# Batch 0's P turned and scaled by one matrix product with a diagonal, and the first layers ranked 16 units later

## The chip, the cores and the metric

One core of one Trainium2 chip runs the whole kernel. The metric is the device time of one execution in microseconds; of three runs of the kernel before, the median was 913.38 us (910.81 to 913.5). TensorE (PE) multiplies matrices, VectorE (DVE) and ScalarE (ACT) work on tiles in SBUF and PSUM, GpSimd (POOL) on tiles in SBUF, SyncE (SP) issues DMAs. PEld is TensorE's loading of the operand that stays in the array while the other one streams through it.

## The reference, cut to what matters

```python
B, H, S, D = 8, 8, 576, 64                    # float32 throughout
scores = q @ k.transpose(0, 1, 3, 2) / sqrt(D)
mask   = (arange(S)//64)[:, None] >= (arange(S)//64)[None, :]
scores = where(mask, scores, -1e9); scores -= scores.max(-1, keepdims=True)
P      = exp(scores); P = P / (P.sum(-1, keepdims=True) + 1e-9)
x      = (P @ v).transpose(0, 2, 1, 3).reshape(4608, 512)
h      = maximum(maximum(x @ w1, x @ w2), x @ w3)      # 512 -> 768
out    = h @ w_out                                     # 768 -> 512
```

## The kernel before

**Attention.** It runs by pairs of heads: 8 batches of 4 pairs, 32 pairs. Of the 576 query rows of a head, tiles t = 0 to 3 hold 128 rows each and see 128(t+1) keys; the last 64 rows of both heads share one tile, p4 (576 keys). A pair takes: first scores of tiles 3, 2 and 0 on TensorE (`qk`, L900, 12 records; a float32 matmul leaves two records), then p4 (`qk4`, L907) and tile 1 (L900 again); the row maximum on VectorE (`top`, L443); exp with row sums on ScalarE (`exp`, L606, and L926 for p4); 1/sum on VectorE (L735, L739; L937, L943 for p4); scaling of P by 1/sum on ScalarE or GpSimd (`normalise`, L459, L461); a turn of P, since the product with v needs keys in the partitions; and P times v (`pv`, L966).

**Batch 0.** The turn has two forms. Batches 1 to 7 transpose 32 x 32 blocks on VectorE (L626) and move them by DMA. Batch 0 (its Part is `PLAIN`) turns q, k (L812) and P (`raise_p` L560, `raise4` L952) on TensorE, in PE's transpose mode, 128 x 128 at a time: 25 such blocks in a pair, 100 in the batch. The result stands in PSUM (tiles named sb, five banks for all of attention) and is copied to the tile pz or pt by ScalarE or VectorE (`copy`, L251 and L253). Scores of one pair want four free banks.

**MoE.** Float32 values are split in a high and a low fp32r part, and each product is three matmuls. x of a batch is split into xh (ScalarE) and xl (GpSimd or VectorE, L256); a chunk is 512 rows, nine of them: one of each batch, and one for the last 64 rows of all. A chunk has 216 matmuls of the first layer (L1089, the maximum at L1102) and 72 of the second (L1123), whose operands are split into tiles hh and hl (slot "hi", three buffers). Weights come as 18 units for the first layer and 6 for the second, and are split on chip: a unit is five VectorE steps (L331, L338, L344, L355, L365), a few ScalarE copies and, in the first 18, four TensorE records (L371, L371, L372, L373).

**Order.** Every step is a `job` with a planner's cost for each engine, a rank and what it waits for. `in_order` plays the jobs through in advance: on every engine the job of the lowest rank that is ready comes first, and that gives each engine's order; the chip then runs it in that order, with waits. A pair of batch 0 is 14 ranks behind the last (`FIRST_PAIR`), later ones 24 (`PAIR`). The first layer of a batch's chunk starts at the rank where the batch's pairs end plus `END`; weight unit u has rank 28 + 3.5 u. Which of two engines takes a copy or a scaling also comes out of this play.

Of the kernel before, what the change touches and what calls it, by code (L numbers as in the profile page):

```python
# [9 lines left out]
F32 = mybir.dt.float32  # L10
# [145 lines left out]
def kernel(  # L156
# [29 lines left out]

    SECOND = 9
    NEAR = 4
    END = 24
    N = 512  # L190

    slots = dict(
# [270 lines left out]
    class Head:  # L463
# [5 lines left out]
        def plan(self, t0):  # L469

            pair, part, self.exps, self.inv = self.pair, self.pair.part, {}, {}
            for n, ts in enumerate(part.groups):
                apart, r = None, t0 + (SECOND if part.beside and ts == part.later else n)
                for t in ts:
                    m = P * (t + 1)
                    d = job(
                        {"DVE": dve(m) + 35.0},
                        r + 1,
                        self.top,
                        t,  # L480
                        after=(pair.scored[ts], apart, pair.began),
                        take=("stat",) if pair.began is None else (),
                    )
                    pair.began = pair.began or d
                    if t != ts[-1]:
                        apart = job({}, 0, lambda eng: None, after=(d,), lasts=GAP)
                    self.exps[t] = job({"ACT": act(m) + 200.0}, r + 2, self.exp, t, after=(d,), take=(f"p{t}",))
                join([self.exps[t] for t in ts], BANK)

        def turns(self, t0, after):  # L490

            pair, part, self.scales = self.pair, self.pair.part, {}
            for t in part.tiles:
                r = t0 + 8 + t / 2 + (SECOND if part.beside and t in part.later else 0)
                self.scales[t] = job(norm_cost(P * (t + 1)), r, self.scale, t, after=(self.inv[t],))
# [13 lines left out]
            return first  # L509

        def plain_turns(self, t0):

            pair, part = self.pair, self.pair.part
            heads, gate = pair.heads, None
            self.placed = []
# [12 lines left out]
            for t in part.tiles:  # L528
                up = job(
                    {"PE": RAISE * (t + 1)},  # L530
                    t0 + 12,
                    self.raise_p,
                    t,
                    after=(self.scales[t], gate),
                    take=("sb",) if gate else ("sb", pair.tag),
                )
                gate = self.gate = gate or up
                join((up,), (f"p{t}",))
                join((place(self.place, t, n=P * (t + 1), after=up),), ("sb",))
            if True:  # L540
                if self.j == 0:
                    pair.raised = [
                        job({"PE": RAISE * n}, t0 + 12, pair.raise4, a, after=(pair.scaled, gate), take=("sb",))
                        for a, n in ((0, 4), (1, 1))
                    ]
                    join(pair.raised, ("p4",))
                for a, n in ((0, 256), (1, 64)):
                    place(self.place4, a, n=n, after=pair.raised[a])
                if self.j == 1:
                    for a in range(2):  # L550
                        join([h.placed[-2 + a] for h in heads], ("sb",))
            self.moved = join(self.placed, ())
# [87 lines left out]
    class Pair:  # L640
# [11 lines left out]
        def plan(self, first, before):  # L652
# [63 lines left out]
            for r, ts in ((first + 7, [t for g in part.first for t in g]), (first + SECOND + 5, part.later)):  # L716
# [10 lines left out]
            join([x for h in self.heads for x in h.scales.values()], ("stat",))  # L727
# [13 lines left out]
        def plan4(self, first, tq, last):  # L741
            asked = job({"ACT": 510.0}, first - TURN + 2, self.ask, after=(tq,), take=("q8",))
            tops = []
            for a in range(2):
                last = job({"PE": 4 * pe(64 if a else 512)}, first + 3 + a, self.qk4, a, after=(asked, last), take=BANK)
                tops.append(
                    job(
                        {"DVE": dve(64 if a else 512) + 65.0},
                        first + 4 + a,
                        self.top4,  # L750
                        a,
# [1 line left out]
                        take=() if a else ("stat4",),  # L753
                    )
                )
            e = job({"ACT": act(512) + act(64) + 350.0}, first + 5, self.exp4, after=tops, take=("p4",), give=2 * BANK)
            inv = job({"DVE": SMALL}, first + 6, self.sum4, after=(e,), lasts=SMALL + GAP)
            inv = job({"DVE": SMALL}, first + 6, self.inverse4, after=(inv,))
            self.scaled = job(norm_cost(S), first + 7, self.scale4, after=(inv,), give=("stat4",))
            join((last,), ("q8",))  # L760
            return last

# [182 lines left out]
        def raise4(self, eng, a):  # L945

            z = self.ps[a] = psa.tile([P, P if a else 512], F32, name="sb")
            for c in range(1 if a else 4):
                src = self.p4[:, c * P : c * P + P]
                if a:  # L950
                    src = self.p4[:, 512:640]
                nc.tensor.transpose(z[:, c * P : c * P + P], src, plus.bitcast(F32))  # L952

        def scale4(self, eng):
            rs = self.stat[2][:, 0:1]
            normalise(eng, self.p4[:, 0:S], rs)
            if self.part.plain:
                nc.gpsimd.tensor_copy(self.p4[:, S:640], self.p4[:, 512:S])

        def pv(self, eng, half):  # L960

# [239 lines left out]
```

## Time and profile before

| | us |
|---|---|
| median of 3 runs (lowest, highest) | 913.38 (910.81, 913.5) |
| profiled execution, its own time | 915.56 |
| its span, first to last instruction | 913.8 |
| TensorE busy in it | 877.1 |
| VectorE busy | 566.3 |
| ScalarE busy | 447.1 |
| GpSimd busy | 184.0 |

Of 36.7 us in which TensorE is not busy, 24.3 lie in the first 103.5 us, where batch 0 runs nearly alone and the weights are split. A busy stretch counts to the modelled end of its last record, so a short burst counts longer than its records hold the array; the distance from start to start is the better price of one record. Clock means the clock granted to TensorE, as a share of 2.4 GHz.

### The profile page before, as it was taken

How to read it: one execution, taken by the hardware profiler on the slowest of the kernel's cores; microseconds unless marked ns; L12 is line 12 of the kernel's file. 1: busy time of each engine (PE TensorE's matmuls, PEld its weight loads, DVE VectorE, ACT ScalarE, POOL GpSimd, SP SyncE). 2: the span in 40 equal slices, each digit the busy share in tenths (PEclk: the TensorE clock that was granted, in tenths of full speed). 3: DMA queues.
4: the chain of work that ended last, by engine and by line, in shares of the span. 5: the costliest groups of instructions: out<-in, count | busy, mean ns of one | idle time of the engine just before them, and what ended most of it. 6: DMA issues, size and time to landing. Idle time of an engine off the chain costs nothing.

```text
span 913.8 us, 13405 instructions
## 1 busy us (share of the span) xinstructions
PE 877.1 (96%) x4336; PEld 643.2 (70%) x4336; DVE 566.3 (62%) x1534; ACT 447.1 (49%) x1227; POOL 184.0 (20%) x232
## 2 busy tenths in 40 slices
PE   5887999998999999999999999999999999999997
PEld 4544566775677777777777777777776778788886
DVE  4988999867767476656675766566656762122121
ACT  5687667655455545545444554545545542113012
POOL 3544213321122112111212121212111210001000
PEclk9998999998999999999999999999999999999999
DMA  5486336655555565546653665266535543000002
GB/s 116 124 230 167 75 83 193 134 133 123 111 114 121 119 138 111 115 97 151 130 111 81 129 141 124 78 131 129 121 96 125 112 86 94 12 1 35 12 1 46
DMA packets 221638, 97.10 MB, mean 106 GB/s; under 512 B 185216, under 2 KB 213888, under 8 KB 221568
## 3 DMA queue, kind: packets, MB, share of 16 engines
q1 hardware_dynamic: 203840, 81.30, 40.2%
q0 software_dynamic: 3456, 12.58, 4.2%
q10 hardware_dynamic: 14272, 2.36, 1.4%
q8 instruction: 34, 0.56, 0.3%
q14 instruction: 36, 0.29, 0.1%
HBM read 40.89 MB, written 9.44 MB: 55 GB/s over the span
## 4 chain that ended last, share of the span: by engine, by line
PE 87%; DVE 8%; ACT 2%; issue 2%; DMA 1%; POOL 0%; ACTq 0%; SPq 0%; DVEq 0%
PE pm L1089 47%; PE pm L1123 16%; PE sb L966 9%; PE sb L900 8%; PE sb L907 3%; DVE sb L443 2%; PE pm L371 1%; PE sb L560 1%; DVE pz L626 1%; DVE wo L344 1%; DVE kq L884 1%; ACT p L606 1%; ACT p L926 1%; DVE wo L338 1%; DVE wo L355 1%
## 5 line engine op out<-in xcount | busy, mean ns | idle before, releaser
L1089 PE MATMUL pm<-xh,w 128*128 128x512 f32 x1296 | 435.8, 405 | 1.0 <-ACT xh L251 1.0
L1089 PEld LDWEIGHTS pm<-xh,w 128*128 128x128 f32 x1296 | 244.7, 189 | 67.2 <-issue 14.1
L1089 PE MATMUL pm<-xl,w 128*128 128x512 f32 x648 | 254.5, 393 | 1.7 <-POOL xl L256 1.7
L606 ACT ACTIVATE p<-sb,nm 128x512 f32<-128x512 f32 (+3 forms) x256 | 133.2, 526 | 100.2 <-DVE nm L443 96.9
L461 POOL TENSOR_TENSOR p<-p,rs 128x128 f32<-128x128 f32 (+3 forms) x138 | 96.7, 724 | 312.5 <-DVE rs L739 265.1
L443 DVE CUSTOM_DVE_ANT_0 sb<-sb,mask 128x512 f32<-128x512 f32 (+3 forms) x288 | 142.9, 528 | 26.5 <-PE sb L907 11.8
L1102 DVE TENSOR_TENSOR m<-pm,m 128x512 f32<-128x512 f32 x108 | 74.1, 686 | 136.8 <-PE pm L1089 136.5
L626 DVE STREAM_TRANSPOSE pz<-p 128x512 f32<-128x512 f32 x280 | 135.7, 523 | 25.6 <-ACT p L459 17.2
L1089 PEld LDWEIGHTS pm<-xl,w 128*128 128x128 f32 x648 | 122.6, 189 | 31.0 <-issue 5.7
L1123 PE MATMUL pm<-wo,hh 128*128 128x512 f32 x432 | 134.5, 393 | 0.4 <-ACT hh L251 0.4
L900 PE MATMUL sb<-kq 64*128 64x128 f32 (+3 forms) x512 | 92.5, 472 | 5.6 <-ACT kq L251 1.8
L966 PE MATMUL sb<-pt,vn 128*64 128x320 f32 (+2 forms) x840 | 92.5, 361 | 3.6 <-issue 2.0
L1123 PEld LDWEIGHTS pm<-wo,hh 128*128 128x128 f32 x432 | 80.1, 188 | 17.7 <-ACT hh L251 0.8
L966 PEld LDWEIGHTS sb<-pt,vn 128*64 128x64 f32 x840 | 56.2, 137 | 44.3 <-issue 11.8
L1123 PE MATMUL pm<-wo,hl 128*128 128x512 f32 x216 | 84.4, 391 | 0.7 <-DVE hl L256 0.7
L900 PEld LDWEIGHTS sb<-kq 64*128 64x128 f32 x512 | 49.2, 192 | 48.1 <-issue 25.0
L251 ACT COPY m<-pm 128x512 f32<-128x512 f32 x54 | 31.6, 586 | 84.5 <-PE pm L1089 84.2
L884 DVE STREAM_TRANSPOSE kq<-nat 128x1152 f32<-128x1152 f32 x28 | 38.5, 1376 | 54.4 <-PE sb L900 53.1
L251 ACT CAST hh<-m 128x384 fp32r<-128x384 f32 x72 | 35.1, 511 | 75.6 <-PE pm L1123 44.2
L459 ACT ACTIVATE p<-p,rs 128x512 f32<-128x512 f32 (+3 forms) x118 | 64.4, 576 | 10.8 <-DVE rs L739 9.7
L256 DVE TENSOR_TENSOR hl<-m,hh 128x384 fp32r<-128x384 f32 x51 | 34.6, 679 | 27.2 <-ACT hh L251 26.2
L606 ACT ACTIVATION_READ_ACCUMULATOR p<-sb,nm 128x1 f32 x256 | 50.7, 198 | 0.0
(86 smaller groups left out, 724.2 us busy)
## 6 DMA issues: line engine op xcount, KB each, us to landing
pt<-pz SPq DMA_DIRECT2D x224, 200.0 KB, 3.9
w<-in_moe_w_dram POOLq DMA_DIRECT2D x18, 512.0 KB, 5.9
vn<-in_v_dram SPq DMA_DIRECT2D x64, 128.0 KB, 2.4
out_dram<-osb SPq DMA_DIRECT2D x32, 256.0 KB, 2.0
nat<-in_k_dram SPq DMA_DIRECT2D x112, 72.0 KB, 2.4
nat<-in_q_dram SPq DMA_DIRECT2D x96, 72.0 KB, 2.4
wo<-in_moe_w_out_dram POOLq DMA_DIRECT2D x6, 512.0 KB, 4.5
nat<-in_q_dram ACTq DMA_DIRECT2D x16, 72.0 KB, 3.3
```

The lines of the kernel that those rows point to most:

```text
L251: nc.scalar.copy(dst, src)
L443: nc.vector.tensor_tensor_reduce(out=ps, in0=ps, in1=hidden, scale=-SCALE, scalar=first, op0=ALU.add, op1=ALU.min, accum_out=out_)
L459: nc.scalar.mul(p, p, r)
L461: nc.gpsimd.tensor_tensor(out=p, in0=p, in1=r.broadcast_to([P, p.shape[1]]), op=ALU.mult)
L606: nc.scalar.activation(dst, src, AF.Exp, bias=nm[:, c : c + 1], scale=-1.0, accum_out=sm[:, c : c + 1])
L626: nc.vector.transpose(dst, p[:, 0 : n * P])
L884: nc.vector.transpose(kq.rearrange("p a s -> p (a s)"), nat.rearrange("p a s -> p (a s)"))
L900: nc.tensor.matmul(ps, self.q[h.own, P * t : P * (t + 1)], self.k[h.own, 0:w], start=True, stop=True)
L966: nc.tensor.matmul(o[h.own].rearrange("p (i u) -> p i u", u=n)[:, :, c0 : c0 + z - a], self.vn[:, kt, h.j, :], h.pt[:, :, a:z], start=(m = ...
L1089: nc.tensor.matmul(self.ps, w[i, f][:, c, :], xx, start=(c == 0 and s == 0), stop=(c == NC - 1 and s == 2))
L1102: nc.vector.tensor_tensor(out=m, in0=ps, in1=m, op=ALU.max)
L1123: nc.tensor.matmul(self.po, h, w[f], start=(f == 0 and s == 0), stop=(f == NF - 1 and s == 2))
```

## The change

In batch 0 no P is scaled any more. Instead a diagonal matrix with 1/sum on its diagonal is made for every tile of rows (`scaling`: the identity `plus` times 1/sum, on VectorE or GpSimd), three tiles of a head or two of tile 1 at a time and one for p4, and P is turned by an ordinary float32 product with it, P being the operand that is loaded: P^T times the diagonal is the turned and scaled P. Four such diagonal jobs stand in a pair. Their tiles are the hh and hl of the MoE's second layer and share its three buffers; a hh goes to the first head and then to tile 1, the hl to the second head. `scale4` keeps only the copy of p4's last 64 columns. The planner's prices change with it: the turn on TensorE costs twice as much, and the maximum and exp, of all batches, cost more (by 121 and 91 ns in `top` and `exp`). `END` goes from 24 to 40. Batches 1 to 7 run the same instructions as before, in another order.

```diff
-    END = 24
+    END = 40
...
-                        {"DVE": dve(m) + 35.0},
+                        {"DVE": dve(m) + 156.0},
...
-                    self.exps[t] = job({"ACT": act(m) + 200.0}, r + 2, self.exp, t, after=(d,), take=(f"p{t}",))
+                    self.exps[t] = job({"ACT": act(m) + 291.0}, r + 2, self.exp, t, after=(d,), take=(f"p{t}",))
...
             pair, part, self.scales = self.pair, self.pair.part, {}
+            if part.plain:
+                return self.plain_turns(t0)
             for t in part.tiles:
...
-            if part.plain:
-                return self.plain_turns(t0)
...
-                    {"PE": RAISE * (t + 1)},
+                    {"PE": 2 * RAISE * (t + 1)},
...
-                    after=(self.scales[t], gate),
+                    after=(pair.diags[t, self.j], gate),
...
-                        job({"PE": RAISE * n}, t0 + 12, pair.raise4, a, after=(pair.scaled, gate), take=("sb",))
+                        job({"PE": 2 * RAISE * n}, t0 + 12, pair.raise4, a, after=(pair.scaled, pair.diags[4, 0], gate), take=("sb",))
...
-                nc.tensor.transpose(z[:, c * P : c * P + P], p[:, c * P : c * P + P], plus.bitcast(F32))
+                nc.tensor.matmul(z[:, c * P : c * P + P], p[:, c * P : c * P + P], self.pair.diag[t, self.j], start=True, stop=True)
...
+            if part.plain:
+                self.diags = {}
+                d = None
+                for n, own in enumerate(([(t, 0) for t in (3, 2, 0)], [(t, 1) for t in (3, 2, 0)], [(1, 0), (1, 1)], [(4, 0)])):
+                    m = P * len(own)
+                    inv = self.inv4 if n == 3 else self.heads[0].inv[own[0][0]]
+                    d = job({"DVE": dve(m), "POOL": pool(m)}, first + 8, self.scaling, n, after=(inv, d), take=("hi",) if n in (0, 2) else ())
+                    self.diags.update(dict.fromkeys(own, d))
...
-            normalise(eng, self.p4[:, 0:S], rs)
             if self.part.plain:
                 nc.gpsimd.tensor_copy(self.p4[:, S:640], self.p4[:, 512:S])
+            else:
+                normalise(eng, self.p4[:, 0:S], rs)
+
+        def scaling(self, eng, n):
...
+            r = r.rearrange("p (n o) -> p n o", o=1).broadcast_to([P, len(own), P])
+            {"DVE": nc.vector, "POOL": nc.gpsimd}[eng].tensor_tensor(out=dst, in0=one, in1=r, op=ALU.mult)
```

TensorE, from the turn of the second pair's q and k (L812, after it L831) to the scores of that pair; L560 and L952 are the turn of the first pair's P, and p_147, p_154, p_164 or p_162, p_202 or p_209 its first head. Before:

```order
L812 MATMUL sb<-plus,nat 128x128 x9
L560 MATMUL sb<-plus,p_147 128x128 x4
L560 MATMUL sb<-plus,p_154 128x128 x3
L560 MATMUL sb<-plus,p_164 128x128
L952 MATMUL sb<-plus,p_170 128x128 x4
L560 MATMUL sb<-plus,p_202 128x128 x2
L952 MATMUL sb<-plus,p_170 128x128
L560 MATMUL sb<-plus,p_157 128x128 x4
L560 MATMUL sb<-plus,p_166 128x128 x3
L560 MATMUL sb<-plus,p_177 128x128
L560 MATMUL sb<-plus,p_207 128x128 x2
L900 MATMUL sb<-kq 128x512 x2
```

The same place after (L564 and L971 are the products, hh and hl the diagonals):

```order
L831 MATMUL sb<-plus,nat 128x128 x9
L564 MATMUL sb<-hh,p_147 128x128 x4
L564 MATMUL sb<-hh,p_154 128x128 x3
L564 MATMUL sb<-hh,p_162 128x128
L564 MATMUL sb<-hl,p_157 128x128 x4
L564 MATMUL sb<-hl,p_166 128x128 x3
L564 MATMUL sb<-hh,p_209 128x128 x2
L971 MATMUL sb<-hh,p_170 128x128 x5
L564 MATMUL sb<-hl,p_177 128x128
L564 MATMUL sb<-hh,p_222 128x128 x2
L919 MATMUL sb<-kq 128x512 x2
```

The 25 blocks of a pair stand in the same gap between two pairs' scores, seven of the second head ahead of tile 1 and p4 now.

GpSimd, from the copy in p4 of the first pair (L958, after it L976) on; L461 scales P, L303 asks for a weight unit. Before:

```order
L958 COPY p_170<-p_170 128x64
L461 TENSOR_TENSOR p_164<-p_164,rs 128x128
L461 TENSOR_TENSOR p_147<-p_147,rs 128x512
L461 TENSOR_TENSOR p_177<-p_177,rs 128x128
L461 TENSOR_TENSOR p_166<-p_166,rs 128x384
L461 TENSOR_TENSOR p_157<-p_157,rs 128x512
L303 DMA w_266<-in_moe_w_dram 128x4x256
```

After (L990 makes a diagonal):

```order
L976 COPY p_170<-p_170 128x64
L990 TENSOR_TENSOR hh<-plus,rs 128x384
L990 TENSOR_TENSOR hl<-plus,rs 128x384
L303 DMA w_254<-in_moe_w_dram 128x4x256
```

Five scalings of P have gone and two diagonals stand in their place, ahead of the second weight unit's request.

TensorE, around the first scores of the fifth pair (the first of batch 1), in the stage of the fourth pair's turn. Before:

```order
L1089 MATMUL pm<-xh_818,w_351 128x512
L900 MATMUL sb<-kq 128x512 x2
L900 MATMUL sb<-kq 128x384 x2
L900 MATMUL sb<-kq 128x128 x2
L371 MATMUL pm<-wo_696,plus 128x512
L372 MATMUL pm<-w_865,osb 128x512
L373 MATMUL pm<-wo_836,plus 128x512
L371 MATMUL pm<-wo_718,plus 128x512
L372 MATMUL pm<-w_885,osb 128x512
L373 MATMUL pm<-wo_869,plus 128x512
L560 MATMUL sb<-plus,p_744 128x128 x4
L560 MATMUL sb<-plus,p_747 128x128 x3
```

After:

```order
L564 MATMUL sb<-hh,p_797 128x128 x2
L371 MATMUL pm<-wo_704,plus 128x512
L372 MATMUL pm<-w_859,osb 128x512
L373 MATMUL pm<-wo_836,plus 128x512
L971 MATMUL sb<-hh,p_848 128x128 x5
L564 MATMUL sb<-hl,p_764 128x128 x4
L564 MATMUL sb<-hl,p_776 128x128 x3
L371 MATMUL pm<-wo_711,plus 128x512
L372 MATMUL pm<-w_904,osb 128x512
L373 MATMUL pm<-wo_889,plus 128x512
L919 MATMUL sb<-kq 128x512 x2
L919 MATMUL sb<-kq 128x384 x2
```

Before, the fifth pair's scores stand ahead of the whole turn of the fourth; after, 22 of the 25 products stand ahead of them.

## Rows read from the trace of the kernel before

**Rows 1.** The page's head and two of its 40 slices' rows.

```profile
span 913.8 us, 13405 instructions
...
PE   5887999998999999999999999999999999999997
...
PEclk9998999998999999999999999999999999999999
```

**Rows 2.** By stage: us, busy time (and records) of each engine, TensorE's clock, DMA.

```profile
0.00:23.90 23.90, 14.02 (x63) 10.01 (x63) 10.24 (x35) 12.52 (x37) 7.42 (x20) 0.93 0.52 123
23.90:62.10 38.20, 30.48 (x184) 18.61 (x184) 34.83 (x102) 28.41 (x84) 18.48 (x23) 1.00 0.68 184
62.10:83.40 21.30, 18.04 (x87) 9.41 (x86) 19.87 (x54) 16.69 (x44) 12.62 (x14) 1.00 0.50 123
83.40:103.50 20.10, 16.64 (x81) 9.69 (x81) 17.26 (x47) 13.79 (x39) 5.44 (x7) 0.83 0.39 120
103.50:134.80 31.30, 30.82 (x139) 20.70 (x135) 30.07 (x74) 19.64 (x48) 4.16 (x5) 1.00 0.42 95
134.80:215.00 80.20, 75.41 (x371) 54.46 (x372) 65.74 (x171) 48.28 (x128) 26.01 (x28) 0.97 0.56 142
215.00:780.00 565.00, 562.82 (x2857) 414.46 (x2856) 360.63 (x1019) 286.13 (x811) 104.83 (x133) 1.00 0.53 116
```

**Rows 3.** TensorE in time, 45 to 62 us and 31 to 33 us.

```profile
53.21 1.82 PE L560 MATMUL sb<-plus,p 128*128 128x128 f32 x12
...
31.58 0.43 PE L907 MATMUL sb<-kq,q 128*128 128x64 f32 x2
31.85 1.08 PE L371 MATMUL pm<-wo,plus 128*128 128x512 f32 x2
```

**Rows 4.** TensorE in time, 4 to 104 us: start, us, what, [idle before].

```profile
19.04 1.97 PE L560 MATMUL sb<-plus,p 128*128 128x128 f32 x8 [2.01 <-POOL p L461]
...
36.01 2.00 PE L900 MATMUL sb<-kq 64*128 64x512 f32 x12 [1.38 <-ACT kq L251]
...
62.10 2.00 PE L900 MATMUL sb<-kq 64*128 64x512 f32 x12
...
74.98 3.02 PE L900 MATMUL sb<-kq 64*128 64x512 f32 x12
...
81.99 0.60 PE L560 MATMUL sb<-plus,p 128*128 128x128 f32 x4
84.25 0.90 PE L560 MATMUL sb<-plus,p 128*128 128x128 f32 x3 [1.66 <-DVE pt L253]
...
93.06 0.38 PE L560 MATMUL sb<-plus,p 128*128 128x128 f32 x2
```

**Rows 5.** Scalings and copies: groups of the first 95 us; GpSimd in time; the page.

```profile
L461 POOL TENSOR_TENSOR p<-p,rs 128x384 f32<-128x384 f32 x5 | 5.0, 1006 | 3.6 <-DVE rs L739 3.6
...
L459 ACT ACTIVATE p<-p,rs 128x512 f32<-128x512 f32 x3 | 2.1, 709 | 0.0
...
L253 DVE COPY pt<-sb 128x512 f32<-128x512 f32 x4 | 2.8, 688 | 0.2 <-PE sb L560 0.2
...
17.58 3.54 POOL L461 TENSOR_TENSOR p<-p,rs 128x128 f32<-128x128 f32 x5
...
L256 DVE TENSOR_TENSOR hl<-m,hh 128x384 fp32r<-128x384 f32 x51 | 34.6, 679 | 27.2 <-ACT hh L251 26.2
```

**Rows 6.** GpSimd in time, 92 to 106 us, and VectorE, 36 to 104 us.

```profile
101.61 1.27 POOL L256 TENSOR_TENSOR xl<-x,xh 128x512 fp32r<-128x512 f32 x1 [2.29 <-ACT xh L251]
...
97.19 0.42 DVE L355 TENSOR_SCALAR wo<-wo 128x512 int32<-128x512 int32 x1
...
101.66 1.50 DVE L355 TENSOR_SCALAR wo<-wo 128x512 int32<-128x512 int32 x1
```

**Rows 7.** As Rows 2, two short stretches of lowered clock.

```profile
84.00:88.00 4.00, 3.75 (x10) 2.36 (x10) 2.34 (x8) 2.68 (x8) 0.31 (x1) 0.50 0.96 325
...
216.00:220.00 4.00, 4.00 (x15) 2.78 (x12) 3.71 (x13) 2.56 (x8) 0.08 (x1) 0.52 0.84 130
```

More of the change, by code (lines that the diff above doesn't have):

```diff
@@ L514, in plain_turns @@
             heads, gate = pair.heads, None
-            self.placed = []
+            self.placed, ups = [], {}
             def place(call, *args, n, after):
@@ L533, in plain_turns @@
                     t,
-                    after=(self.scales[t], gate),
+                    after=(pair.diags[t, self.j], gate),
                     take=("sb",) if gate else ("sb", pair.tag),
                 )
-                gate = self.gate = gate or up
+                gate, ups[t] = gate or up, up
                 join((up,), (f"p{t}",))
@@ L551, in plain_turns @@
                         join([h.placed[-2 + a] for h in heads], ("sb",))
+            self.ups = ups
+            if self.j == 1:
+                join([x for h in heads for x in h.ups.values()] + pair.raised, ("hi",))
+                join([h.ups[t] for h in heads for t in (3, 2, 0)], ("hi",))
             self.moved = join(self.placed, ())
@@ L726, in plan @@
                 turn = h.turns(first + 4 * j, turn)
-            join([x for h in self.heads for x in h.scales.values()], ("stat",))
+            if part.plain:
+                join(set(self.diags.values()), ("stat", "stat4"))
+            else:
+                join([x for h in self.heads for x in h.scales.values()], ("stat",))
             if not part.plain:
@@ L747, in plan4 @@
                     job(
-                        {"DVE": dve(64 if a else 512) + 65.0},
+                        {"DVE": dve(64 if a else 512) + 156.0},
                         first + 4 + a,
@@ L755, in plan4 @@
                 )
-            e = job({"ACT": act(512) + act(64) + 350.0}, first + 5, self.exp4, after=tops, take=("p4",), give=2 * BANK)
+            e = job({"ACT": act(512) + act(64) + 530.0}, first + 5, self.exp4, after=tops, take=("p4",), give=2 * BANK)
             inv = job({"DVE": SMALL}, first + 6, self.sum4, after=(e,), lasts=SMALL + GAP)
             inv = job({"DVE": SMALL}, first + 6, self.inverse4, after=(inv,))
-            self.scaled = job(norm_cost(S), first + 7, self.scale4, after=(inv,), give=("stat4",))
+            self.inv4 = inv
+            if self.part.plain:
+                self.scaled = job({"POOL": pool(64)}, first + 7, self.scale4, after=(e,))
+            else:
+                self.scaled = job(norm_cost(S), first + 7, self.scale4, after=(inv,), give=("stat4",))
             join((last,), ("q8",))
@@ L951, in raise4 @@
                     src = self.p4[:, 512:640]
-                nc.tensor.transpose(z[:, c * P : c * P + P], src, plus.bitcast(F32))
+                nc.tensor.matmul(z[:, c * P : c * P + P], src, self.diag[4, 0], start=True, stop=True)
         def scale4(self, eng):
             rs = self.stat[2][:, 0:1]
-            normalise(eng, self.p4[:, 0:S], rs)
             if self.part.plain:
                 nc.gpsimd.tensor_copy(self.p4[:, S:640], self.p4[:, 512:S])
+            else:
+                normalise(eng, self.p4[:, 0:S], rs)
+        def scaling(self, eng, n):
+            if not hasattr(self, "diag"):
+                self.diag = {}
+            tag, own = (("hh", [(t, 0) for t in (3, 2, 0)]), ("hl", [(t, 1) for t in (3, 2, 0)]), ("hh", [(1, 0), (1, 1)]), ("", [(4, 0)]))[n]
+            if tag:
+                self.d = moe.tile([P, 3, P], F32, name=tag, bufs=slots["hi"])
+            dst = self.d[:, 0 : len(own)] if tag else self.d[:, 2:3]
+            r = (self.stats[2][:, 0, 0:3], self.stats[2][:, 1, 0:3], self.stats[2][:, :, 3], self.stat[2][:, 0:1])[n]
+            one = plus.bitcast(F32).rearrange("p (o n) -> p o n", o=1).broadcast_to([P, len(own), P])
+            r = r.rearrange("p (n o) -> p n o", o=1).broadcast_to([P, len(own), P])
+            {"DVE": nc.vector, "POOL": nc.gpsimd}[eng].tensor_tensor(out=dst, in0=one, in1=r, op=ALU.mult)
+            for m, key in enumerate(own):
+                self.diag[key] = dst[:, m]
         def pv(self, eng, half):
```

## The prediction, made before the changed kernel ran

> **What bounds the kernel now.** I read the 40 slices first: TensorE is full from about the ninth slice on and thin only ahead of it [rows 1]. By stages, it is busy 562.8 of 565 us from 215 to 780, so whatever is added to TensorE there costs its whole length, and what is taken off other engines there is worth nothing [rows 2]. What can move lies ahead of 215: TensorE stands idle 9.9 us up to 23.9, 7.7 up to 62.1, 3.3 up to 83.4, 3.5 up to 103.5, 0.5 up to 134.8 and 4.8 up to 215 [rows 2], 29.6 in all. About 9 of the first 9.9 are the loads and the lone chain of the first pair and stay. From 23.9 to 134.8 the busiest other engine is VectorE: 102.0 of 110.9 us [rows 2]. It splits the weights and feeds the pairs, so the front is a race between VectorE's queue and each pair's chain, with TensorE third. Two stretches also run at half clock, 1.2 GHz: around 84 to 88, after a thin stretch with two transposes' bursts and a 1.66 us gap, and around 216 to 220 [rows 4, 7]. The stage's mean of 0.83 over 20.1 us means 6.8 us at half clock, up to 3.4 us lost; 0.97 over 80.2 means 4.8 us, up to 2.4 lost [rows 2].
>
> So the sum is: time = TensorE's work + TensorE's idle time + what half clock takes.
>
> **Change, part one: 100 turns become 100 products.** A transpose of 128 columns is one record; twelve in a row take 1.82 us, the last of which lasts 0.27 to its end, so (1.82 - 0.27)/11, about 0.14 us from start to start, and 0.11 to 0.13 in other bursts; I take 0.125 [rows 3]. A product is two records with two weight loads. No row of before shows it with 128 columns. The nearest is p4's product with 64 columns on a full 128 x 128 operand: two records from 31.58 to 31.85, 0.27 us [rows 3]. From below, a product with four passes over 128 columns at 2.4 GHz is 0.21; from above, if nothing overlapped, 0.27 plus another 64 columns in four passes, 0.107, is 0.38. I take 0.27, the row's own value, since weights seem to hold it there and not columns. The term is 100 x (0.27 - 0.125) = **+14.5 us** of TensorE work, between +9 and +25. All of it falls ahead of about 90 us.
>
> The Trainium skill speaks against this change: "Perfetto Trace Analysis", section on transposes, says a logical transpose should be a transpose and not a standard matmul, and "TensorE: Matmul & The Clock Gate", section on terms, calls the transpose mode four times faster for FP32. By that a product would be 4 x 0.125 = 0.5 us, an estimate, and the term +37.5; the 0.27 of the row speaks against so much.
>
> **Part two: the scaling goes.** ScalarE loses 15 scalings of 128 to 576 columns, at 0.71 for 512 about 9 us [rows 5]. GpSimd loses 21 scalings, 6,848 columns, at 1.01 for 384 about 18 us, and gets seven diagonals of 384 and one of 256 columns, 7.7 us: 10 less [rows 5]. VectorE gets eight diagonals, 1,664 columns; its nearest row is a two-input operation of 384 columns in 0.68, so +2.9 us [rows 5]. None of this lies on TensorE. It matters by three roads.
>
> First, ScalarE's free time takes copies out of PSUM from VectorE: in the two orders VectorE copies 4,480 columns less in batch 0; at 0.69 for 512 that is 6.0 us off the busiest feeder, net 3.1 less after its diagonals [rows 5].
>
> Second, VectorE stalls beside GpSimd: the same weight step takes 0.42 alone and 1.50 where a GpSimd operation of 1.27 begins just ahead of it [rows 6]. With 10 us less of GpSimd work in this stage, and only a part of VectorE's steps of that kind, I take 2 to 4 us.
>
> Third, the chain of a pair. In the first pair GpSimd scales from 17.58, behind a copy that itself waited for ScalarE's scaling of p4, and the turn begins at 19.04 [rows 4, 5]. Now one diagonal of about 1 us is enough for eight products, and the copy has nothing to wait for: about 18.2.
>
> **Walking the pairs** (estimates from these prices and the two orders). First pair: 18.2 + 25 x 0.27 = 25.0 against 23.9, so the second pair's scores come 1.1 later. Second pair: its diagonal is VectorE's, right behind 1/sum; products from about 34 or 35 to 43; but 18 of them stand ahead of the third pair's scores, which go from 36.0 to about 41 [rows 4]. Third pair: its turn about 52 to 60, where twelve of its transposes ran at 53.2 [rows 3]; the fourth pair's scores at about 61 against 62.1 [rows 4]. Fourth pair: two diagonals on GpSimd, no scaling in VectorE's shadow: products from about 75 against 81.99, done by 85 to 88 against 93.4; the fifth pair's scores, which stood at 74.98 ahead of the turn, at about 84 to 87 [rows 4]. At that point all 14.5 us have been paid, and apart from them TensorE stands about where it stood before at 83.4: idle time covers them. I don't trust such a walk to leave so few gaps and leave 2 us uncovered: **+14.5 - 12.5**. Without that cover, that is if the chains were as long as before, the full 14.5 would show.
>
> What was in 83.4 to 103.5 is then gone in the main: the fourth pair's turn, with its 1.66 us wait for a free bank behind VectorE's copies, is over. The stage's 3.5 us idle and up to 3.4 of half clock become VectorE's and TensorE's common pace of the next stage, in which nearly nothing is idle [rows 2, 4]. I take **-4** of 6.9. TensorE half clock came after thin bursts here; the Trainium skill ("TensorE: Matmul & The Clock Gate", part on transposes) adds that transposes don't count as activity for the clock as matmuls do, by which the stretch would vanish for certain; the trace can't tell that from the gaps beside it.
>
> **Part three: END.** The first layers move 16 ranks back, two thirds of a pair: in the two orders, by the thirteenth pair 384 matmuls of the first layer stand ahead of its scores instead of 432. The 48 others move from beside attention into the tail, where TensorE is as full [rows 1]; so that costs nothing. It can help where chunk 1 starts: there x has hardly been split when its products come up, and the gaps and half clock at 208 to 220 follow [rows 7]. Of 4.8 idle and 2.4 of clock from 134.8 to 215, and the rest of the half clock behind it, I take **-2**, since new gaps come with a new order [rows 2]. The second layer's hh and hl share their buffers with the diagonals, but the second layer of the first chunk needs all its first layer ahead of it, when the last diagonal is long used up: no cost. The changed prices of maximum and exp alter nothing but order. Requests for weights on GpSimd move from behind five scalings to behind two diagonals, earlier by 1.5 us for the second unit [rows 5]; none is waited for.
>
> **Sum**, against the profiled span: 913.8 + 14.5 - 12.5 - 4 - 2 = 909.8, 4.0 less. That execution took 915.56 in all, 1.8 more than its span and 2.2 above the median of 913.38; the difference carried over to the median gives **909.4 us**.
>
> **Rivals.** (1) VectorE sets the pace alone: its 102 of 110.9 us mean that TensorE's waits only change their names, the weights end when they did, and diagonals and stalls eat what the copies gave [rows 2]. Then the 14.5 vanish in idle time, but nothing is won: 912.5 to 914, no change. For it speaks VectorE's share; against it that it loses 3 us net and some stalls.
> (2) Slower: a product costs 0.38, not 0.27. The turn then takes 9.5 us of each pair, TensorE becomes the bound between 18 and 85, and the further 10.7 us have no cover: about 920. From about 0.33 a product the gain is gone, from 0.35 the kernel is slower than can be mistaken. For it: two loads of 128 columns per product, which the trace can't split from the streaming. Against it: 0.27 for the 64-column product.
> (3) Products at 0.5, as the rule on transposes would have it: 23 more than forecast, 932. Nothing in the rows asks for it.
> (4) The new order takes the gaps from 134.8 to 220 and most of 83 to 103: 9 to 10 of the 14 us there instead of 6, and pair chains as walked: 902 to 905.
>
> **How the numbers follow.** A measurement of this kernel can tell about 0.3%, 2.7 us, from no change; that is below 910.6 or above 916.1. Forecast (906 to 912.5): 0.45, of which 0.32 lies below 910.6. Rival 4: 0.17, faster. Rival 1: 0.18, nearly all without change, 0.05 slower by a little. Rival 2: 0.16, slower. Rival 3: 0.04, slower. Faster 0.50, same 0.25, slower 0.25. The range, 901 to 920, takes in rivals 4, 1 and most of 2 and leaves out 3 and the far ends.
>
> **What would show it.** Products about 0.27 us from start to start, 100 of them in 27 us, else term one is wrong. The four pairs' first products at about 18, 35, 52 and 75, and the fifth pair's scores at 84 to 87: if these come 5 us later, the cover is missing. The last of the 18 weight units' sums on TensorE some 2 us earlier than before. VectorE's steps of 0.42 stalled less often. The clock at 1.00 between 80 and 104. From 220 to the end, nothing but the shift should differ; if the time moved there, the walk of the front explains nothing.

## The result, and the profile after

The changed kernel takes **899.81 us** (median of 4 runs, 898.59 to 902.51) against 912.74 (4 runs, 910.81 to 913.5): ratio 0.9866, 95% interval 0.9836 to 0.9895, 12.9 us less. The forecast was 909.4, and its range began at 901. The sign was right; the size was wrong by a factor of three, and a large part of the gain lies where the prediction said that nothing could move.

Four lines of the page of the kernel after, as in [rows 1]:

```profile
span 896.5 us, 13559 instructions
...
PE 872.5 (97%) x4436; PEld 647.8 (72%) x4436; DVE 562.3 (63%) x1533; ACT 442.0 (49%) x1241; POOL 172.2 (19%) x199
...
PE   6998899999999999999999999999999999999997
...
PEclk9999999999999999999999999999999999999999
```

The profiled executions differ by 17.3 us of span (913.8 and 896.5, the latter from 898.59 us in all), more than the medians. The granted clock differs between executions of one kernel: 17 of the kernel before, run beside later experiments, took 908.7 us at a mean clock of 0.996 up to 915.62 at 0.985, so what follows on the clock holds for these two executions. Of the 17.3 us TensorE's idle time gives 12.7 (36.7 before, 913.8 less the 877.1 busy us of its page; 24.0 after), and 4.6 are less *busy* time, though 100 records were added. The stages after, with the bounds and columns of [rows 2], and the tail:

```profile
0.00:23.90 23.90, 15.90 (x96) 11.88 (x98) 11.78 (x41) 12.55 (x38) 5.57 (x17) 1.00 0.62 143
23.90:62.10 38.20, 36.04 (x244) 25.55 (x241) 32.20 (x102) 29.54 (x86) 13.62 (x17) 1.00 0.68 185
62.10:83.40 21.30, 17.95 (x111) 12.09 (x110) 19.03 (x53) 15.09 (x42) 8.97 (x11) 1.00 0.64 165
83.40:103.50 20.10, 16.70 (x78) 9.01 (x77) 18.34 (x51) 14.47 (x39) 7.35 (x9) 0.95 0.41 83
103.50:134.80 31.30, 31.30 (x142) 21.24 (x141) 28.86 (x75) 18.27 (x45) 5.70 (x7) 0.98 0.46 101
134.80:215.00 80.20, 78.05 (x391) 57.43 (x391) 64.30 (x180) 52.88 (x143) 26.92 (x28) 1.00 0.64 158
215.00:780.00 565.00, 565.00 (x2897) 419.11 (x2894) 362.94 (x1000) 279.05 (x814) 99.02 (x108) 1.00 0.51 112
780.00:920.00 140.00, 111.56 (x491) 91.47 (x489) 24.87 (x36) 20.12 (x38) 5.02 (x4) 0.99 0.06 15
```

Against [rows 2], 7.4 us of idle time have gone ahead of 62.1, 3.1 from 103.5 to 215, and 2.2 behind it; 62.1 to 103.5 kept its 6.7. Half clock (1.2 GHz) has nearly gone: by the stages' means it held for 3.3 + 6.8 + 4.8 = 15 us up to 215 before, and 3.8 of the four behind 216 [rows 2, 7]; now 2.0 + 1.3 = 3.3 us by the same reading of the stages from 83.4 to 134.8. That gives back up to half of 15.5 us, nearly 8, of TensorE's *busy* time, about what the products added (7.7 us by the groups below).

One place, which overlaps with these sums, stands out: the start of the second chunk (the prediction counts from 0 and calls it chunk 1). The stretch from 200 to 220 us, before:

```profile
200.00:220.00 20.00, 17.36 (x81) 11.05 (x81) 12.12 (x37) 10.39 (x29) 3.45 (x4) 0.83 0.40 92
```

and after:

```profile
200.00:220.00 20.00, 20.00 (x107) 14.33 (x106) 12.70 (x38) 11.34 (x33) 2.55 (x3) 1.00 0.66 159
```

Before, 2.6 us were idle and 0.17 x 20 = 3.4 us went to half clock, some 6 in all; after, neither is left.

The rest of the gain is told best by the chunks. A chunk's second layer ends at these rows, and the next chunk begins behind them. TensorE in time, before:

```profile
398.28 0.39 PE L1123 MATMUL pm<-wo,hl 128*128 128x512 f32 x1
...
402.09 0.50 PE L1089 MATMUL pm<-xh,w 128*128 128x512 f32 x1
...
416.72 3.79 PE L966 MATMUL sb<-pt,vn 128*64 128x320 f32 x28
...
492.67 0.39 PE L1123 MATMUL pm<-wo,hl 128*128 128x512 f32 x1
```

and after (L1157 is L1123's line now, L1123 is L1089's, L1000 is L966's):

```profile
393.93 0.39 PE L1157 MATMUL pm<-wo,hl 128*128 128x512 f32 x1
394.16 0.33 PE L926 MATMUL sb<-kq,q 128*128 128x64 f32 x2
394.30 0.48 PE L1123 MATMUL pm<-xh,w 128*128 128x512 f32 x1
...
396.54 2.93 PE L1000 MATMUL sb<-pt,vn 128*64 128x320 f32 x28
...
487.23 0.39 PE L1157 MATMUL pm<-wo,hl 128*128 128x512 f32 x1
```

From chunk to chunk it took 492.67 - 398.28 = 94.39 us and takes 93.30. Of the 1.09 us, 0.86 stand in one row: the 28 products of P and v of a batch's first pair took 3.79 us and take 2.93. That row counts as busy throughout, but the weight loads under it stood still. TensorE's weight loads before, here and two chunks on:

```profile
416.72 0.19 PEld L966 LDWEIGHTS sb<-pt,vn 128*64 128x64 f32 x2 [0.35 <-issue]
417.59 2.68 PEld L966 LDWEIGHTS sb<-pt,vn 128*64 128x64 f32 x26 [0.68 <-issue]
...
607.13 1.47 PEld L966 LDWEIGHTS sb<-pt,vn 128*64 128x64 f32 x13 [1.39 <-DMA pt<-pz]
```

and after:

```profile
396.54 2.69 PEld L1000 LDWEIGHTS sb<-pt,vn 128*64 128x64 f32 x28 [0.35 <-issue]
```

The gap of 0.35 ahead of the row is there in both; the one of 0.68 is not. At 607.13 the view names what ended it: the DMA that brings the second head's turned P (`pt<-pz`). At 417.59 it only says "issue", but the packed trace holds the wait itself: in TensorE's queue an instruction of L966 waits for two semaphores from 415.83 to 417.56, one of them that of the last `pt<-pz` transfer, whose last packet landed at 417.53, and the load starts at 417.59. Such gaps, of 0.7 to 1.4 us, stand at 323.18, 512.00, 607.13 and 702.12 too, each behind such a wait. In the changed kernel there is none from 310 to 785.

So a stage that was "562.8 of 565 busy" held some 1 us of stall in each batch, a wait for P. Over the four periods from the second chunk's end to the sixth's, 378.5 us have become 372.7, 5.7 less.

### The profile page after: what moved, and what is told of

It reads as the page before. It is cut to its first block, busy times and chain, and to the rows that moved or that the text cites. A ratio compares the mean times of both kernels' runs of the same rounds, so it can differ in the third digit from the quotient of the medians.

```text
span 896.5 us, 13559 instructions
## 1 busy us (share of the span) xinstructions
PE 872.5 (97%) x4436; PEld 647.8 (72%) x4436; DVE 562.3 (63%) x1533; ACT 442.0 (49%) x1241; POOL 172.2 (19%) x199
## 4 chain that ended last, share of the span: by engine, by line
PE 85%; DMA 1%; DVE 1%; ACT 0%; issue 0%; POOL 0%; ACTq 0%
PE pm L1123 49%; PE pm L1157 17%; PE sb L1000 9%; PE sb L919 7%; PE sb L926 3%; DMA wo<-in_moe_w_out_dram 1%; PE pm L371 0%; DVE wo L344 0%; DMA nat<-in_q_dram 0%; DMA vn<-in_v_dram 0%; DVE kq L903 0%; ACT wo L326 0%; DVE rs L750 0%; PE pm L373 0%; PE pm L372 0%
## 5 line engine op out<-in xcount | busy, mean ns | idle before, releaser
L1123 PE MATMUL pm<-xh,w 128*128 128x512 f32 x1296 | 434.2, 403 | 0.0
L1123 PEld LDWEIGHTS pm<-xh,w 128*128 128x128 f32 x1296 | 244.1, 188 | 65.0 <-issue 13.1
L1123 PE MATMUL pm<-xl,w 128*128 128x512 f32 x648 | 253.7, 392 | 0.9 <-POOL xl L256 0.9
L1123 PEld LDWEIGHTS pm<-xl,w 128*128 128x128 f32 x648 | 122.3, 189 | 28.3 <-issue 4.8
L1157 PE MATMUL pm<-wo,hh 128*128 128x512 f32 x432 | 136.0, 396 | 0.4 <-ACT hh L251 0.4
L461 POOL TENSOR_TENSOR p<-p,rs 128x256 f32<-128x256 f32 (+3 forms) x91 | 71.6, 805 | 312.4 <-DVE rs L754 278.2
L1157 PEld LDWEIGHTS pm<-wo,hh 128*128 128x128 f32 x432 | 80.6, 188 | 20.1 <-issue 1.5
L919 PE MATMUL sb<-kq 64*128 64x128 f32 (+3 forms) x512 | 88.1, 459 | 3.2 <-ACT p L945 1.6
L1000 PE MATMUL sb<-pt,vn 128*64 128x320 f32 (+2 forms) x840 | 90.4, 361 | 0.5 <-DMA pt<-pz 0.4
L1000 PEld LDWEIGHTS sb<-pt,vn 128*64 128x64 f32 x840 | 56.5, 137 | 39.2 <-issue 8.9
L1157 PE MATMUL pm<-wo,hl 128*128 128x512 f32 x216 | 84.4, 391 | 0.0
L459 ACT ACTIVATE p<-p,rs 128x384 f32<-128x384 f32 (+3 forms) x133 | 64.9, 540 | 34.3 <-DVE rs L754 34.3
L919 PEld LDWEIGHTS sb<-kq 64*128 64x128 f32 x512 | 45.5, 187 | 43.9 <-issue 21.3
L256 POOL TENSOR_TENSOR hl<-m,hh 128x384 fp32r<-128x384 f32 x19 | 19.9, 1050 | 171.3 <-ACT hh L251 150.2
```

What stands on the lines that cost most here:

```text
L256: {"DVE": nc.vector, "POOL": nc.gpsimd}[eng].tensor_tensor(out=dst, in0=a, in1=b, op=ALU.subtract)
L459: nc.scalar.mul(p, p, r)
L461: nc.gpsimd.tensor_tensor(out=p, in0=p, in1=r.broadcast_to([P, p.shape[1]]), op=ALU.mult)
L919: nc.tensor.matmul(ps, self.q[h.own, P * t : P * (t + 1)], self.k[h.own, 0:w], start=True, stop=True)
L1000: nc.tensor.matmul(o[h.own].rearrange("p (i u) -> p i u", u=n)[:, :, c0 : c0 + z - a], self.vn[:, kt, h.j, :], h.pt[:, :, a:z], start=(m = ...
L1123: nc.tensor.matmul(self.ps, w[i, f][:, c, :], xx, start=(c == 0 and s == 0), stop=(c == NC - 1 and s == 2))
```

## The experiments

The change has three parts: products with diagonals in place of scaling; END from 24 to 40; and new prices of maximum and exp in the planner. **Theory at first:** the front's parts give little, and END, with or without the prices, gives most, batch by batch. **Rival:** the products and the freed engines give it, and END only a little where the second chunk starts (the prediction's chunk 1), as the prediction had it. The two edits that are taken in and out:

```diff
-    END = 24
+    END = 40
```

```diff
-                        {"DVE": dve(m) + 35.0},
+                        {"DVE": dve(m) + 156.0},
...
-                    self.exps[t] = job({"ACT": act(m) + 200.0}, r + 2, self.exp, t, after=(d,), take=(f"p{t}",))
+                    self.exps[t] = job({"ACT": act(m) + 291.0}, r + 2, self.exp, t, after=(d,), take=(f"p{t}",))
...
-                        {"DVE": dve(64 if a else 512) + 65.0},
+                        {"DVE": dve(64 if a else 512) + 156.0},
...
-            e = job({"ACT": act(512) + act(64) + 350.0}, first + 5, self.exp4, after=tops, take=("p4",), give=2 * BANK)
+            e = job({"ACT": act(512) + act(64) + 530.0}, first + 5, self.exp4, after=tops, take=("p4",), give=2 * BANK)
```

**END alone**, on the kernel before.

> The kernel before with END at 40 and nothing else. Front theory (the gain comes from the shorter turn chains of batch 0, as the prediction had it, and END is worth 2 us): 909 to 913. Order theory (END takes away the wait of one P-times-v per batch, 0.9 us in the steady batches, and the gaps and half clock at 208 to 220): 900 to 905, with a period of about 93.3 us from batch to batch instead of 94.4, and batch 0's stage as before.

904.66 us (902.02 to 906.65), ratio 0.9922 [0.9904, 0.9940]: 7.4 less, as the order theory had it. The periods from the second chunk's end to the sixth's are 92.9 to 94.9 us, not 93.3 each time.

**Prices alone**, on the kernel before.

> The kernel before with the planner's higher prices of maximum and exp (156 and 291 instead of 35 and 200, and those of p4) and nothing else; END 24, transposes, scaling. Front and order theory both: 909 to 915, since the prices only shuffle the order. A third theory, that the dearer prices give the order that no longer waits: 900 to 906, with the period of 93.3 us.

930.93 us, ratio 1.0211 [1.0194, 1.0229]: 18.9 more, the largest effect of any part taken alone, from numbers that cost no instruction. None of the three theories had that.

**The changed kernel without its END** (24).

> The changed kernel with END back at 24; TensorE's first 137 rows of order are those of the changed kernel. Front theory: 899 to 903. Order theory: 906 to 911, the period again 94.4 us, a front up to 120 us like the changed kernel's.

923.79 us (922.34 to 931.4), ratio 1.0153 [1.0124, 1.0183]. Both theories missed it: they had left the prices out.

**The changed kernel with the old prices** (END 40).

> The changed kernel with the old prices of maximum and exp; END 40, products and diagonals stay. Front and order theory: 898 to 903, as the changed kernel. Price theory: 905 to 912.

902.85 us (899.7 to 906.5), ratio 0.9909 [0.9886, 0.9932]: within 898 to 903.

**END and prices without the products.**

> The kernel before with END 40 and the new prices, but with transposes and scaling: what the changed kernel is without products and diagonals. If these are worth what they were with the old prices (902.85 against 904.66): 901 to 903. If worth what they were at END 24 (923.79 against 930.93): 905 to 908. If they cost: below 899.

900.53 us (899.3 to 904.58), ratio 0.9892 [0.9865, 0.9919]. Without any product, nearly the whole gain is there; the time is half a microsecond under the first expectation.

**Products alone** (END 24, old prices).

> Products and diagonals on the kernel before, END 24, old prices. Front theory: 899 to 903. Order theory: 905 to 912, a gain of 2 to 7 at the most, the steady batches 94.4 us apart as before.

908.82 us (12 runs), ratio 0.9971 [0.9954, 0.9989]: 3.1 less, as the order theory had it.

With the kernels before and after these six fill the table of all eight combinations (us, medians; the kernel before as it ran beside the first four):

| | END 24, old prices | END 24, new prices | END 40, old prices | END 40, new prices |
|---|---|---|---|---|
| transposes | 912.0 | 930.9 | 904.7 | 900.5 |
| products | 908.8 | 923.8 | 902.9 | 899.8 |

Products: -0.7 to -7.1, of which -0.7 can't be told from nothing (899.3 to 904.58 and 898.59 to 902.51 overlap). END: -6 to -7 with the old prices, -24 to -30 with the new. Prices: +15 to +19 at END 24, -3 to -4 at END 40, which is near what can be told apart, but of one sign in both rows.

**What a product costs** was measured by itself, in two kernels. The first is the changed kernel with transposes in place of products; the diagonals are still made, but not used, and P of the first batch stays unscaled. Of its two places the one for p4 (L971; L564 is changed in the same way):

```diff
-                nc.tensor.matmul(z[:, c * P : c * P + P], src, self.diag[4, 0], start=True, stop=True)
+                nc.tensor.transpose(z[:, c * P : c * P + P], src, plus.bitcast(F32))
```

> The changed kernel with the order left as it is, each product replaced by a transpose of the same block; the diagonals are still made, but not used, so batch 0's P stays unscaled. Measures the price of the products: at 0.22 us against 0.125 TensorE has 9.8 us less work. If the work lies on the path: 889 to 892. If the front's other waits take it: 896 to 900.

896.28 us (894.14 to 897.19), ratio 0.9834 [0.9809, 0.9859]. Against END and prices alone (900.53), freeing the engines from scaling, with the order that goes with it, is worth about 4.3 us; the products take 3.5 of them back. The groups of transposes take 13.2 + 3.4 = 16.6 us in this kernel, those of products 27.0 in the changed one (below): of 10.4 us more work about 7 were covered by other waits, within the second expectation (896 to 900).

The second writes each product twice, at the same two places.

```diff
-                nc.tensor.matmul(z[:, c * P : c * P + P], src, self.diag[4, 0], start=True, stop=True)
+                for _ in range(2):
+                    nc.tensor.matmul(z[:, c * P : c * P + P], src, self.diag[4, 0], start=True, stop=True)
```

> The changed kernel with every product written twice to the same place: 22.3 us more of TensorE work in the first 85 us. On the path: 918 to 922. Half covered by waits: 909 to 912.

919.44 us, ratio 1.0094 [1.0070, 1.0118]: 19.6 above the changed kernel. By the two pages TensorE is busy 894.2 instead of 872.5 us, 0.217 a product. Of 21.7 us added on top, about 2 were covered: the waits that could hide such work were nearly used up by the first writing.

**Why END pays in every batch.** The trace of the changed kernel at END 24 shows it. (The execution that was profiled took 931.4 us; the median is 923.79.) TensorE in time where a chunk begins:

```profile
403.63 0.39 PE L1157 MATMUL pm<-wo,hl 128*128 128x512 f32 x1
...
404.00 0.48 PE L1123 MATMUL pm<-xh,w 128*128 128x512 f32 x1
...
408.94 0.49 PE L1123 MATMUL pm<-xh,w 128*128 128x512 f32 x1 [0.51 <-ACT xh L251]
410.28 0.50 PE L1123 MATMUL pm<-xl,w 128*128 128x512 f32 x1 [0.85 <-POOL xl L256]
...
411.61 3.56 PE L919 MATMUL sb<-kq 64*128 64x512 f32 x12 [0.60 <-DVE kq L903]
...
500.82 0.39 PE L1157 MATMUL pm<-wo,hl 128*128 128x512 f32 x1
```

ScalarE there, splitting x of the batch's last pair, and the stage by window (columns of [rows 2]):

```profile
408.27 0.62 ACT L251 CAST xh<-x 128x512 fp32r<-128x512 f32 x1
```

```profile
411.00:415.00 4.00, 3.40 (x13) 1.74 (x12) 3.37 (x11) 2.03 (x6) 0.61 (x1) 0.57 0.48 79
```

The first layer begins at 404.00, but its last quarter of x is copied only at 408.27 and its remainder is made behind that. TensorE waits 0.51 + 0.85 us for these and 0.60 for the turned k and q of the next pair, then runs at a granted clock of 0.57, at half clock for most of the four us: twelve scores take 3.56 us instead of 2.00 [rows 4]. That is 3.5 of the 3.9 us by which this chunk is longer (97.19 against 93.30). It recurs at each start; TensorE's waits from 310 to 785 in this kernel, us in all, times, longest:

```profile
PE pm L1123 <- POOL xl L256: 4.2, 5, 0.8
PE sb L919 <- DVE kq L903: 3.0, 5, 0.6
PE pm L1123 <- ACT xh L251: 2.6, 5, 0.5
...
```

The changed kernel has no wait in that stretch. The kernel with the new prices alone has the same three waits there, five times each (4.3, 2.9 and 2.6 us), and periods of 96.6 to 97.3 us. With the old prices x is not late at END 24, only the turned P above. In the kernel before, ScalarE makes this copy at the last moment, while TensorE's first product stands at 402.09:

```profile
402.00 0.62 ACT L251 CAST xh<-x 128x512 fp32r<-128x512 f32 x1
```

and in the changed kernel all four are made 20 us ahead of the first product at 394.30:

```profile
374.27 2.17 ACT L251 CAST xh<-x 128x512 fp32r<-128x512 f32 x4
```

END thus sets how long the first layer of a batch stands behind the chain of its last pair. With 24, the length of one pair, there is no slack; with 40 there are some 16 us (16 ranks of 0.97 us). This is **theory A**: a threshold. Theory B is a gain in proportion to the ranks. Four kernels tell them apart, the changed one with END 32, 48, 56, and with 24 for two chunks only:

```diff
-        starts.append(rank + END)
+        starts.append(rank + (24 if b < 2 else END))
```

> The changed kernel with END = 32, half of the way back to 24. Theory A (a batch's first layer waits for its own last pair: with END 24 the split of x ends just as its products come up; a rank lasts about 0.97 us in a steady batch, 93.3 us for 96 ranks, so 8 ranks are 7.8 us of slack and the waits at a chunk's start are below 1.2 us each): the loss of 24.0 us from END 40 to 24 is gone nearly whole, 898 to 904 us, periods of 93.3 to 94.0 us from chunk to chunk, no half clock after 300. Theory B (the gain of END is in proportion to the ranks that the first layer moves, since work moves from one full stretch into another): half of the loss, 911 to 912 us, periods near 95.5.

902.38 us (900.78 to 903.95), ratio 0.9907 [0.9883, 0.9930]; from the third chunk's end to the sixth's 94.2, 93.3 and 93.3 us, and no half clock behind 300.

> The changed kernel with END = 48. Theory A: the slack is already enough at 40, so the steady periods stay 93.3 us and the time changes only by what the front loses or gains when the first chunk starts 8 ranks later: 897 to 903 us. Theory B: another gain of some 12 us, 888 us.

901.75 us (900.11 to 903.21), ratio 0.9895 [0.9872, 0.9917]; there 93.5 each time.

> The changed kernel with END = 56. Theory A: steady periods 93.3 us as at 40; the first chunk starts 16 ranks later, and the stretch from 103 to 215 has 48 matmuls fewer to fill its gaps, so 899 to 908 us. Theory B: 876 us.

903.75 us (902.28 to 905.43), ratio 0.9916 [0.9894, 0.9938]. From the third chunk's end on 97.0, 93.4 and 93.4 us; the 97.0 misses the expectation, but that period holds 512 matmul records where the next has 477. The first chunk ends at 210.9 us, not 205.1, and 5.5 of these 5.8 us are still there at the last second-layer product (897.1, not 891.6).

> The changed kernel with END = 24 for the first two chunks and 40 from the third on. Theory A (END pays once per batch, at every chunk's start): chunk by chunk it follows the kernel with 24 up to the end of the second chunk (205.3, 305.1 us) and has periods of 93.3 from the third or fourth on; it keeps the 4 to 10 us lost there and ends 904 to 910 us, against 923.8 with 24 throughout and 899.8 with 40. Rival C, the reason given in the prediction (END matters where chunk 1 starts, around 208 to 220, and nowhere else): the loss stays, 918 us or more.

904.74 us (901.19 to 906.41), ratio 0.9925 [0.9899, 0.9950]. Ends of the chunks (last second-layer product of each, us):

| chunk | 1 | 2 | 3 | 4 | 5 | 6 |
|---|---|---|---|---|---|---|
| END 24 throughout | 205.3 | 305.1 | 403.6 | 500.8 | 598.5 | 696.3 |
| END 24 for two, then 40 | 197.1 | 299.6 | 396.9 | 490.1 | 583.4 | 676.7 |
| END 40 throughout | 205.1 | 301.1 | 393.9 | 487.2 | 580.5 | 673.8 |

The last kernel loses while END is 24 (102.4 and 97.3 us from end to end) and runs at 93.3 from the next chunk on. Its first chunk ended 8 us before that of END 24, though the order on every engine is the same in both up to 249 us; what differs there is the execution of END 24 in the first row, which ran at half clock for 17 us ahead of 205 (this one for none from 10 to 204) and took 7.6 us more than its kernel's median. The first row's ends are late by about that much, and the expectation that this kernel follows END 24 holds for its order up to there. The times fit theory A in all four kernels, B in none, and rival C, by which the place that the prediction named is the only one, falls (918 or more expected for the last). TensorE's busy time from 310 to 785 in four kernels says the same, columns as in [rows 2]. Before:

```profile
310.00:785.00 475.00, 472.81 (x2402) 349.44 (x2400) 299.20 (x843) 238.43 (x676) 86.41 (x110) 1.00 0.52 115
```

the changed kernel with END 24:

```profile
310.00:785.00 475.00, 464.14 (x2324) 339.06 (x2325) 297.85 (x851) 246.42 (x698) 75.06 (x86) 0.98 0.51 114
```

with END 32:

```profile
310.00:785.00 475.00, 474.85 (x2416) 351.74 (x2413) 288.08 (x820) 240.65 (x676) 70.25 (x81) 1.00 0.50 110
```

and as it is, with 40:

```profile
310.00:785.00 475.00, 475.00 (x2418) 352.63 (x2417) 297.15 (x815) 226.04 (x659) 82.41 (x88) 1.00 0.49 109
```

No kernel with all of the work beats the changed one; those with 32 to 56 lie within 4 us of it.

**What stays open.** Why higher prices make x later at END 24 (in the copy above 4.3 us behind the start of the chunk, against level with it at the old prices) wasn't traced through the planner. Nor was it shown why the turned P of a batch's first pair is late at END 24 and the old prices: that it is the same lack of slack is argued only. The experiments show it as far as this: with END 40 and nothing else, of the five gaps from 310 to 785 one is left (1.3 us, at 420.0); with products, END 24 and the old prices the view names the same wait:

```profile
PE sb L1000 <- DMA pt<-pz: 2.5, 2, 1.4
```

## Why the prediction was wrong, point by point

**Reading the bound: failed.** "Whatever is added to TensorE there costs its whole length" may stand, but "what can move lies ahead of 215" doesn't follow from 562.8 of 565 us. Busy time counts a row whose loads stall and a row at half clock as busy. The number of records shows it: 2,857 in [rows 2], 2,897 in the same 565 us now. The weight loads show it too: 414.46 us of them in [rows 2], 419.11 now, 1.1% more, where the period fell by 1.2%. The Trainium skill ("Perfetto Trace Analysis", section on identifying the most-contended engine) says that matmul busy time is a poor measure of how near a kernel is to its limit, and that the busy share of weight loads is a better one; the trace agrees (73% before, 74% after), and the prediction had passed that rule over.

**Part one: the product was mis-sized.** Groups by line of the whole kernel, after:

```profile
L564 PE MATMUL sb<-hh,p 128*128 128x128 f32 x96 | 13.2, 279 | 4.7 <-POOL hh L990 2.3 <-DVE stat L956 1.7 <-DVE hh L990 0.7
L564 PE MATMUL sb<-hl,p 128*128 128x128 f32 x64 | 8.7, 277 | 0.0
...
L971 PE MATMUL sb<-hh,p 128*128 128x128 f32 x40 | 5.1, 275 | 0.0
```

and before:

```profile
L560 PE MATMUL sb<-plus,p 128*128 128x128 f32 x80 | 14.8, 313 | 9.7 <-POOL p L461 2.9 <-DVE pt L253 2.5 <-DVE pz L253 1.8
...
L952 PE MATMUL sb<-plus,p 128*128 128x128 f32 x20 | 4.5, 347 | 0.5 <-ACT p L459 0.5
```

In an undisturbed burst four products take 0.89 us from start to start (33.26 to 34.15 below), 0.22 each, not 0.27. The row that gave 0.27 was no measure: the same two records of 64 columns take 0.14 at 394.16 above. Against 0.125 for a transpose the term is +9.7, the lower end of its range of +9 to +25, and not +14.5; the two kernels with the same order gave 10.4 of busy time. In groups by line the 100 products take 13.2 + 8.7 + 5.1 = 27.0 us, which is the forecast's 27 by chance, since a group counts to the modelled ends; the 100 transposes took 19.3, split into small groups and in part at half clock, so in these two executions the difference was +7.7. Rivals 2 (0.38) and 3 (0.5) fall with 0.22.

**Parts two and walk: right within 6 us.** TensorE in time, after, at the first products of the four pairs and the fifth pair's scores:

```profile
16.64 2.05 PE L564 MATMUL sb<-hh,p 128*128 128x128 f32 x16 [0.78 <-POOL hh L990]
...
32.19 1.13 PE L564 MATMUL sb<-hh,p 128*128 128x128 f32 x8 [0.65 <-DVE hh L990]
...
33.26 1.06 PE L564 MATMUL sb<-hh,p 128*128 128x128 f32 x8
34.15 1.06 PE L564 MATMUL sb<-hl,p 128*128 128x128 f32 x8
...
48.99 2.01 PE L564 MATMUL sb<-hh,p 128*128 128x128 f32 x16
...
71.41 2.05 PE L564 MATMUL sb<-hh,p 128*128 128x128 f32 x16 [1.56 <-POOL hh L990]
...
81.06 2.00 PE L919 MATMUL sb<-kq 64*128 64x512 f32 x12
```

16.6, 32.2, 49.0, 71.4 and 81.1 against 18, 35, 52, 75 and 84 to 87: each 1.4 to 6 us early, the more the later, as smaller products would have it. VectorE was busy 98.4 us from 23.9 to 134.8, 3.6 less than before, where the forecast had 3.1 and some stalls. The weights' last sums came 2.0 us earlier (132.5 for 134.5), as forecast. The front's net, +14.5 - 12.5 - 4 = -2, measured -3.1 alone and -0.7 beside the other parts: right in its sum, which is luck, since the sizes of its terms were off. The cover in particular was some 7 us and not 12.5, and beyond the products' own work it was nearly nothing: of the doubled products' 21.7 us about 2 were hidden. From 83.4 to 103.5 the idle time stayed (3.46, now 3.40), and only the clock gave something (0.83, now 0.95).

**Part three: the step that failed.** "Of 4.8 idle and 2.4 of clock from 134.8 to 215 ... I take -2": END measured -7.4 alone, and -11.4 with the prices, each against the kernel before beside it. The kind of mechanism named there, a chunk's work that comes up before what it needs is ready, was right. Its size was not, even at the place it named: from 200 to 220 some 6 us went in the profiled executions, not 2. And each later batch, put at nothing, has such a place too, with END no longer than PAIR: with the new prices x is late there, with the old ones the turned P of the first pair, 1.1 us in a period of 94.4. "The changed prices of maximum and exp alter nothing but order" was true and no argument: that order is worth +15 to +19 us at END 24 and -3 to -4 at END 40. The text's own test, "if the time moved there [from 220 on], the walk of the front explains nothing", decided against it.

**Rivals.** Rival 4 (902 to 905) came nearest in time and in cause, a new order that takes gaps, but had them ahead of 220. Rival 1, no gain, has the number of the products beside the other two parts (-0.7); whether VectorE set the pace there wasn't tested.

## What to carry to other kernels

In a loop that repeats, compare the period with the work of one turn (records, weight loads), not with a busy share: here about one microsecond of hidden stall in each batch came to 5.7 us over four periods, where the products in the front gave 3.1 alone. Where a view says "issue", look in the trace for a wait instruction in the queue just ahead. Where one number sets how far a consumer stands behind the last producer of its batch, look for the last producer's end and the consumer's start in the trace; level with each other means no slack, and any other change of order, even of a planner's prices alone, can then cost 2%. Test the parts of a change together and apart: the prices were worth -3 to -4 or +15 to +19 us by the value of another constant.

## What the runs showed of the hardware

A float32 product of 128 x 128 blocks with 128 columns cost 0.22 us in bursts and 0.217 by the doubled kernel. A transpose cost 0.11 to 0.14: four in 0.60 us, the last 0.27 to its end, make 0.11 from start to start [rows 4], and twelve in 1.82 make 0.14 [rows 3]. That is a factor of 1.6 to 2. The Trainium skill ("TensorE: Matmul & The Clock Gate", section on terms) calls the transpose mode four times faster for FP32; the measured factor is smaller, and it decides here.

Half clock didn't follow the turn. Slices of TensorE's clock in the changed kernel with the old prices, all products (an execution of 906.5 us, the longest of its six):

```profile
PEclk8999799999999999999999999999999999999999
```

and in the one that turns by transposes, which has the new prices:

```profile
PEclk9999999999999999999999999999999999999999
```

The changed kernel itself has products and the same order as the second, and its slices are all 9 too: it ran at half clock for 3.4 us, the one with transposes for 6.8, each in one execution. So neither kind of turn goes with the lower clock here. The Trainium skill ("TensorE: Matmul & The Clock Gate", part on PE-mode transpose) has it that transposes don't count as busy in the same way; these runs don't decide that. In the traces read closely the lowered clock stood behind gaps in TensorE's work, as at 411 above.
